# Transposes, values and scores of a tile as one group on TensorE, with attention further ahead

## The chip, the cores and the metric

The kernel runs on one core of a Trainium2 chip. The time is device microseconds of one execution, taken as the median of several runs; lower is better. The engines of a core work side by side, each on its own queue in order: TensorE (PE; its weight loads are listed apart as PEld), VectorE (DVE), ScalarE (ACT), GpSimd (POOL) and SyncE (SP), which here only issues loads. [...]

## The reference

An attention over 4 batches, 8 heads, 768 positions and a head size of 64, in which each query sees the 31 keys nearest to it and, for each of the 24 blocks of 32 positions, one key (the maximum over the block) and one value (the mean). Its output is the input of a two-layer network over 3072 tokens.

```python
k_sum = k.reshape(B, H, nb, block, D).max(axis=3)
v_sum = v.reshape(B, H, nb, block, D).mean(axis=3)
scores_l = scale * np.matmul(q, k.transpose(0, 1, 3, 2))
mask_l = np.abs(pos[:, None] - pos[None, :]) < window
scores_s = scale * np.einsum('bhsd,bhnd->bhsn', q, k_sum) + np.log(block)
a = softmax(concat(where(mask_l, scores_l, -1e9), scores_s))
x = matmul(a, concat(v, v_sum))              # to (3072, 512)
h = x @ w_in                                 # (3072, 1024)
solu = h * softmax(h)
ln = (solu - mean) / sqrt(var + 1e-6) * g_ln
out = ln @ w_out                             # (3072, 512)
```

All is in float32.

## The kernel before

**Tiles and steps.** The network's tokens go in 24 tiles of 128 (t = 0 to 23). Attention goes in 12 pieces (batch b, piece g of 256 queries) of two steps each (pp = 0 or 1, four heads each), 24 steps in all, so one step for a tile of the network; a piece with both of its steps is the input of two tiles. Names in the views carry these numbers: `s2_1_0` is the scores of b = 2, g = 1, pp = 0, and `h12` belongs to tile 12. Steps and tiles are counted from 0.

**Products on TensorE.** For a step: `s`, the scores (16 products in two passes, 32 records of 64x120); `t`, 16 transposes of the normalised weights `e`; `x`, the values (32 records). For a tile: `h` (24 products of 128x512, from the high and low parts `xh`, `xl` of x and of `w_in`), `lt` (16 transposes of the normalised hidden layer `he`) and `o` (24 products of 128x512 with `w_out`). `h` and `o` are called the large products below, the others the small ones. `vs_ps` holds the block means of a batch's values.

**Between them.** Scores: VectorE adds the mask and takes the maximum (8 instructions, `e`, `nm`), ScalarE exponentiates (8 instructions), ScalarE and VectorE make the reciprocal `z`, VectorE or GpSimd multiplies (`e<-e,z`). Transposes `t` are copied to `at` (two copies), `x` to `xh` with a subtraction into `xl`. Hidden layer: VectorE takes the maximum (`hm`), ScalarE exponentiates (`he`, `hz`), VectorE multiplies (`he<-h,hz,he`, the last reader of `h`), then follow mean, variance and a power on GpSimd (`y`). `lt` is copied to `lh`, with a subtraction into `ll`, in two halves each.

**Buffers.** In PSUM `h` has one buffer; `s`, `t`, `lt` and the block means share two in turn; `x` and `o` share two in turn. In SBUF `qt`, `vt`, `kw`, `e`, `at`, `xh`, `lh` have two each and `kraw` three.

**What sets the order.** The kernel is written as a list of operations (`plan.op`), each with a cost, its engines and what it reads and writes. `Plan.issue` then plays a schedule with these costs, takes at each point the operation that can start first (of equals the one that is due first), and issues the instructions in that order, which each engine keeps. So a line that moves in the loop changes the order of all engines. An operation enters the list of those ready when what it depends on has ended, plus `SYNC` (0.13). `run` takes several generators and makes one TensorE operation of their first products. The loop over t (line 724) puts, for a tile, the values and scores of a coming step, the loads (`load_q`, `load_v`, `load_keys`), the first layer (`first`), the transposes (`turn`, `values_turn`), four stages of splitting `w_out` for the first tiles, and the second layer of tile t - 3 (`LAG`). From t = `NEAR` = 4 on the transposes of both kinds go in one `run`, and values and scores in another.

Early on VectorE, ScalarE and GpSimd also split the two weight matrices into high and low parts (`raw`, `cv_in`, `cv_out`, `w`) and form block maxima (`ksum`) and block sums (`st_v`, `vacc`) of the coming batches.

## Time and profile before

| | us |
|---|---|
| median of 3 runs | 418.68 (418.41 to 419.27) |
| the profiled execution | 419.72 |
| its span | 417.9 |
| TensorE, products busy | 396.2 |
| VectorE busy | 284.1 |
| ScalarE busy | 243.6 |
| GpSimd busy | 124.2 |

The profiled execution gives one record for each instruction, with its start, its length and what ended the idle time ahead of it. Ends of products are modelled, so two large products that follow each other overlap in the records, and distances are best read from start to start. A row of the timeline joins neighbours of a kind; `x32` is their count, and a bracket names the idle time ahead of the row and what ended it. The granted clock is TensorE's, 1.00 at full speed.

### The profile page before, as it was taken

What the parts mean: (1) busy time and instruction counts of PE and PEld (TensorE: products, weight loads), DVE (VectorE), ACT (ScalarE), POOL (GpSimd) and SP (SyncE); (2) the same over time, 40 slices, a digit from 0 to 9 for tenths busy, and PEclk for the clock granted to TensorE, in tenths of its full rate; (3) what the DMA queues carried; (4) which work ended last, traced back from release to release, by engine and by line L of the source; (5) the groups of instructions that cost most, each with busy time, mean ns of one, the idle gap of its engine ahead of it and who ended that gap; (6) DMA issues with size and microseconds to landing.
All of it is one profiled execution on the core that took longest, in us unless ns stands there. A gap on an engine that the chain in (4) does not pass through costs nothing.

```text
span 417.9 us, 9489 instructions
## 1 busy us (share of the span) xinstructions
PE 396.2 (95%) x3667; PEld 299.3 (72%) x3667; DVE 284.1 (68%) x841; ACT 243.6 (58%) x710; POOL 124.2 (30%) x172
## 2 busy tenths in 40 slices
PE   7999598889899999999999999999999999999996
PEld 3437376567678777777877777777777777777876
DVE  4998899996877776736876764564676567453440
ACT  4967889737556745745763673675675566332231
POOL 4676546887851101108102110110110100111010
PEclk9999879999999999999999999999999999999999
DMA  8999996428337412126134220241230000000011
GB/s 268 410 256 263 327 245 164 127 78 197 91 117 200 130 49 80 52 88 153 55 100 124 77 78 27 76 102 40 77 95 29 25 6 23 27 25 2 25 50 52
DMA packets 22929, 46.03 MB, mean 110 GB/s; under 512 B 1860, under 2 KB 8260, under 8 KB 22884
## 3 DMA queue, kind: packets, MB, share of 16 engines
q1 hardware_dynamic: 18096, 36.97, 31.4%
q10 hardware_dynamic: 4788, 8.46, 6.2%
q8 instruction: 29, 0.48, 0.5%
q14 instruction: 16, 0.13, 0.1%
HBM read 36.97 MB, written 6.29 MB: 104 GB/s over the span
## 4 chain that ended last, share of the span: by engine, by line
PE 58%; DMA 16%; DVE 15%; ACT 5%; POOL 3%; issue 1%; SPq 0%; DVEq 0%
PE h L616 26%; PE o L681 22%; DMA kraw<-in_k 4%; DMA vt<-in_v 4%; DMA raw<-in_w_out 4%; DVE hm L623 3%; DVE e L518 3%; DVE he L629 3%; ACT he L625 3%; PE x L590 3%; PE lt L552 3%; DMA st_v<-in_vb 2%; PE t L552 2%; PE s L498 2%; POOL st_v L418 2%; DMA raw<-in_w_in 2%
## 5 line engine op out<-in xcount | busy, mean ns | idle before, releaser
L616 PE MATMUL h<-w,xh 128*128 128x512 f32 x384 | 141.1, 405 | 8.2 <-DVE he L629 6.9
L681 PE MATMUL o<-w,lh 128*128 128x512 f32 (+1 forms) x400 | 142.4, 394 | 0.1
L616 PEld LDWEIGHTS h<-w,xh 128*128 128x128 f32 x384 | 72.4, 189 | 31.8 <-issue 11.0
L681 PEld LDWEIGHTS o<-w,lh 128*128 128x128 f32 x400 | 74.1, 188 | 19.0 <-issue 2.9
L681 PE MATMUL o<-w,ll 128*128 128x512 f32 (+1 forms) x200 | 77.2, 386 | 0.5 <-DVE ll L666 0.5
L616 PE MATMUL h<-w,xl 128*128 128x512 f32 x192 | 75.7, 394 | 0.0
L526 ACT ACTIVATE e<-e,nm 128x120 f32<-128x120 f32 x192 | 73.0, 384 | 1.1 <-DVE nm L518 1.1
L636 POOL TENSOR_SCALAR he<-he,nmu 128x512 f32<-128x512 f32 x27 | 23.8, 883 | 99.5 <-DVE nmu L632 99.3
L625 ACT ACTIVATE he<-h,hm 128x1024 f32<-128x1024 f32 x24 | 26.7, 1114 | 42.9 <-DVE hm L623 42.8
L238 ACT COPY at<-t 120x512 f32<-120x512 f32 x45 | 24.2, 587 | 41.5 <-PE t L552 41.4
L681 PEld LDWEIGHTS o<-w,ll 128*128 128x128 f32 x200 | 37.6, 188 | 8.0 <-DVE ll L666 0.8
L518 DVE CUSTOM_DVE_ANT_0 e<-s,mask 128x120 f32<-128x120 f32 x192 | 40.5, 275 | 2.8 <-PE s L498 2.8
L616 PEld LDWEIGHTS h<-w,xl 128*128 128x128 f32 x192 | 36.3, 189 | 6.8
L623 DVE TENSOR_REDUCE hm<-h 128x1 f32<-128x1024 f32 x24 | 29.3, 1221 | 14.9 <-PE h L616 14.9
L240 POOL COPY kw<-ksum 128x192 f32<-128x192 f32 (+1 forms) x26 | 9.4, 363 | 100.6 <-PE s L498 79.9
L641 ACT ACTIVATE sq<-he 128x1024 bf16<-128x1024 f32 x24 | 25.4, 1057 | 22.6 <-POOL he L636 20.6
L239 DVE CAST lh<-lt 128x512 fp32r<-128x512 f32 x23 | 15.8, 687 | 32.4 <-PE lt L552 27.1
L666 DVE TENSOR_TENSOR ll<-lt,lh 128x512 fp32r<-128x512 f32 x48 | 31.8, 684 | 8.5 <-ACT lh L238 8.1
L418 POOL TENSOR_TENSOR st_v<-st_v 96x512 f32<-96x512 f32 (+3 forms) x42 | 33.9, 816 | 8.8 <-DMA st_v<-in_vb 6.3
L526 ACT ACTIVATION_READ_ACCUMULATOR e<-e,nm 128x1 f32 x192 | 36.3, 189 | 0.0
L590 PEld LDWEIGHTS x<-at,vt 120*64 120x64 f32 (+1 forms) x768 | 25.4, 141 | 10.4 <-issue 5.2
L629 DVE SCALAR_TENSOR_TENSOR he<-h,hz,he 128x1024 f32<-128x1024 f32 x24 | 30.7, 1278 | 0.2
(79 smaller groups left out, 525.3 us busy)
## 6 DMA issues: line engine op xcount, KB each, us to landing
vt<-in_v SPq DMA_DIRECT2D x12, 768.0 KB, 5.8
kraw<-in_k SPq DMA_DIRECT2D x16, 400.0 KB, 7.5
out<-os ACTq DMA_DIRECT2D x23, 256.0 KB, 2.0
qt<-in_q SPq DMA_DIRECT2D x11, 512.0 KB, 4.0
st_v<-in_vb SPq DMA_DIRECT2D x12, 384.0 KB, 3.7
raw<-in_w_in SPq DMA_DIRECT2D x8, 512.0 KB, 7.1
raw<-in_w_out SPq DMA_DIRECT2D x8, 512.0 KB, 12.0
vt<-vsum ACTq DMA_DIRECT2D x11, 192.0 KB
```

Of the source, the lines that this page charges most:

```text
L238: by = {act: lambda: nc.scalar.copy(out=to(), in_=of()), dve: lambda: nc.vector.tensor_copy(out=to(), in_=of()), pool: lambda: nc.gpsimd.t ...
L418: op(pool, 0.15 + w * 0.0021, lambda w=w, o=o: nc.gpsimd.tensor_tensor(out=o.ap[:n, :w], in0=x.ap[:n, :w], in1=x.ap[:n, w:2 * w], op=ALU.add),
L518: nc.vector.tensor_tensor_reduce(out=e.ap[:, n, :], in0=sc.ap[:, j, (2 * i + up) * KC:(2 * i + up + 1) * KC], in1=mask[:, mi, :], scale=-S ...
L526: nc.scalar.activation(out=e.ap[:, n, :], in_=e.ap[:, n, :], func=AF.Exp, bias=nm.ap[:, n:n + 1], scale=-1.0, accum_out=z.ap[:, n:n + 1])
L590: nc.tensor.matmul(xp.ap[j * D:(j + 1) * D, i, qs], vs.ap[:k, u, cs], at.ap[:k, u % 2, n[j] + u // 2, :], start=not apart, stop=not apart ...
L616: nc.tensor.matmul(o, a.ap[:, c, ts], w.ap[:, i], start=(c == 0 and n == 0), stop=(c == NKC - 1 and n == 2))
L623: op(dve, 1.13, lambda: nc.vector.tensor_reduce(out=nm.ap, in_=h.ap, op=ALU.max, axis=AX.X, negate=True), r=[h], w=[nm])
L625: op(act, 1.09, lambda: nc.scalar.activation(out=e.ap, in_=h.ap, func=AF.Exp, bias=nm.ap, accum_out=z.ap), r=[h, nm], w=[e, z])
L629: op(dve, 1.27, lambda: nc.vector.scalar_tensor_tensor(out=e.ap, in0=h.ap, scalar=z.ap, in1=e.ap, op0=ALU.mult, op1=ALU.mult, accum_out=s1 ...
L641: op(act, 1.13, lambda: nc.scalar.activation(out=sq.ap, in_=e.ap, func=AF.Square, accum_out=ss.ap), r=[e], w=[sq, ss])
L666: op(dve, 0.6, lambda part=part, r=r: nc.vector.tensor_tensor(out=part(lo), in0=tp.ap[:, r], in1=part(hi).bitcast(F32), op=ALU.subtract), ...
L681: nc.tensor.matmul(o.ap[:, cols], a.ap[:, f, :], w.ap[:, i, cols], start=(f == 0 and n == 0), stop=(f == NFC - 1 and n == 2))
```

## The change

The switch `NEAR` goes from 4 to 6. Up to it, scores, transposes and values of a step each are an operation of their own. From tile 6 on a tile's small products are put in this order: transposes of step t + 3 (`values_turn`), transposes of tile t - 2 together with the values of step t + 2, and the scores of step t + 4. They are chained: each carries `then`, the operation that TensorE has to take next, so that nothing comes in between, and the first waits for what the second needs. Scores were one pair of tiles ahead and are now two, and the loads of queries (`load_q`) and keys (`load_keys`, at tables `load_at` and `blocks_at`) are asked for at other tiles. In `Plan.issue` an operation of TensorE that follows one of TensorE no longer has `SYNC` added before it is ready.

```diff
@@ -37,7 +37,7 @@
 NT = B * S // P
 LAG = 3
 NHE = 4
-NEAR = 4
+NEAR = 6
 WPT = 2
 
 
@@ -64,6 +64,7 @@
     def __init__(self, can, deps, prio, nbytes, port):
         self.can, self.deps, self.engine, self.fn, self.port = can, deps, None, None, port
         self.prio, self.nbytes, self.end, self.start, self.users, self.left = prio, nbytes, None, None, [], 0
+        self.then = None
 
 
 class Plan:
@@ -128,7 +129,7 @@
         return o
 
     def issue(self):
-        ready, free, dma = {}, {}, 0.0
+        ready, free, then, dma = {}, {}, {}, 0.0
         for o in self.ops:
             o.left = len(o.deps)
             for d in o.deps:
@@ -138,8 +139,9 @@
             if "sp" in o.can:
                 o.due = o.prio
 
-        def enter(o, at):
+        def enter(o):
             for e in o.can:
+                at = max((d.end + (0.0 if d.engine == e == "pe" else self.SYNC) for d in o.deps), default=0.0)
                 ready.setdefault(e, []).append((at, o))
 
         def begin(e, at):
@@ -154,6 +156,8 @@
 
         def take(e):
 
+            if e in then:
+                return next(((begin(e, at), o) for at, o in ready[e] if o is then[e]), None)
             best = None
             for at, o in ready[e]:
                 t = begin(e, at)
@@ -173,13 +177,16 @@
 
         for o in self.ops:
             if not o.left:
-                enter(o, 0.0)
+                enter(o)
         order = []
         while len(order) < len(self.ops):
             t, e, o = min(((x[0], e, x[1]) for e in ready for x in [take(e)] if x),
                           key=lambda x: (x[0], x[2].due))
             for f in o.can:
                 ready[f] = [x for x in ready[f] if x[1] is not o]
+            then.pop(e, None)
+            if o.then:
+                then[e] = o.then
             o.start, o.engine, (o.cost, o.fn) = t, e, o.can[e]
             o.end = free[e] = t + cost(e, o, t)
             if o.nbytes:
@@ -189,7 +196,7 @@
             for u in o.users:
                 u.left -= 1
                 if not u.left:
-                    enter(u, max(d.end for d in u.deps) + self.SYNC)
+                    enter(u)
         at, done = self.START, set()
         for o in order:
             if o.engine == "pe":
@@ -541,8 +548,10 @@
             cost, fns, r, w = zip(*(x for _, x in mine))
             op(pe, sum(cost) - 0.25 * (len(mine) - 1), lambda: [f() for f in fns],
                r=[x for y in r for x in y], w=[x for y in w for x in y])
+            done = plan.ops[-1]
         for f, _ in mine:
             assert next(f, None) is None
+        return done if mine else None
 
     def turn_halves(to, of):
 
@@ -721,30 +730,57 @@
     for f in range(NFC):
         load_w_out(f, ())
     rows = [(hh, i) for hh in range(2) for i in range(2)]
+
+    load_at, blocks_at = ((0, 1, 2, 3), (-1, 0, 1, 1)), ((0, 1, 2, 3), (0, 1, 1, 2))
+
+    def pairs(at, t):
+        return [(b + 1, p) for b in range(B - 1) for p in range(NPAIR) if t == 2 * NG * b + at[b > 0][p]]
+
+    step = lambda i: (*its[i // 2], i % 2)
     for t in range(NT):
         n, j = divmod(t, 2)
         b, g = its[n]
-        nxt = its[n + 1] if n + 1 < len(its) else None
-        near, before = t >= NEAR, its[(t + 1) // 2:(t + 1) // 2 + 1]
-        run(*[values(*x, (t - 1) % 2) for x in before if near], *([scores(*nxt, j)] if nxt else []))
+        near = t >= NEAR
+        if not near:
+            run(scores(*step(t + 2)))
+
+        if t == NEAR - 1 or (near and j == 0 and n + 3 < len(its)):
+            load_q(*its[n + 3])
+        elif j == 0 and not near:
+            load_q(*its[n + 2], after=begun if n == 0 else ())
         if j == 0 and n + 2 < len(its):
-            load_q(*its[n + 2], after=begun if n == 0 else ())
             load_v(*its[n + 2], after=begun if n == 0 else ())
-        if b + 1 < B and g < 2:
-            load_keys(b + 1, 2 * g + j, begun if n < 2 else ())
+        for p in pairs(load_at, t):
+            load_keys(*p, begun if t < 4 else ())
         first(t)
         rows_behind = [turn(t - LAG + 1)] if t > LAG - 2 else []
-        run(*([values_turn(*nxt, j)] if nxt and near else []), *rows_behind)
+        if near:
+            parts = [run(values_turn(*step(t + 3)))] if t + 3 < NT else []
+            parts.append(run(*rows_behind, *([values(*step(t + 2))] if t + 2 < NT else [])))
+            if t + 4 < NT:
+                parts.append(run(scores(*step(t + 4))))
+
+
+            for x, y in zip(parts, parts[1:]):
+                x.then = y
+                y.deps.add(x)
+            parts[0].deps.update(*[y.deps - {parts[0]} for y in parts[1:2]])
+        else:
+            run(*rows_behind)
         for f in range(WPT * t, min(WPT * t + WPT, NFC)):
             split_w_out(f)
         if t > LAG - 1:
             second(t - LAG)
         if not near:
-            run(values_turn(*nxt, j))
-            if t + 1 < NEAR:
-                run(values(*nxt, j))
-        if b + 1 < B and g < 2:
-            key_blocks(b + 1, 2 * g + j)
+            run(values_turn(*step(t + 2)))
+            if t == NEAR - 1:
+                run(scores(*step(t + 3)))
+            run(values(*step(t + 2)))
+            if t == NEAR - 1:
+                run(values_turn(*step(t + 3)))
+                run(scores(*step(t + 4)))
+        for p in pairs(blocks_at, t):
+            key_blocks(*p)
 
         if b + 1 < B and (g < 2 if b else g == 1):
             for r in [2 * g + j] if b else [2 * j, 2 * j + 1]:
```

Three places show what that does to the order. The first is TensorE around the transposes of tile 11 (`lt11`), behind the last products `h13`, where each tile from 7 to 19 looks alike. Before, in the order of issue:

```order
L616 MATMUL h13_3022<-w5_509,xh2_0_2620 128x512
L552 MATMUL t2_1_1_3065<-ident_66,e2_1_1_2977 120x64 x16
L552 MATMUL lt11_3082<-ident_66,he11_2780 128x64 x16
L616 MATMUL h13_3022<-w7_533,xh2_0_2620 128x512
L616 MATMUL h13_3022<-w7_533,xl2_0_2647 128x512
L616 MATMUL h13_3022<-w7_533,xh2_0_2620 128x512
L681 MATMUL o10_3107<-w8_724,lh10_2918 128x512
L681 MATMUL o10_3107<-w8_724,ll10_2924 128x512
L681 MATMUL o10_3107<-w8_724,lh10_2918 128x512
L590 MATMUL x2_1_1_3114<-at2_1_1_3102,vt2_1_2420 64x64 x16
L498 MATMUL s2_2_0_3131<-kw2_2_0_2792,qt2_2_2622 64x120 x16
L681 MATMUL o10_3107<-w9_740,lh10_2918 128x512
```

TensorE in the changed kernel, at the same `lt11`:

```order
L625 MATMUL h13_3084<-w7_533,xl2_0_2681 128x512
L625 MATMUL h13_3084<-w7_533,xh2_0_2661 128x512
L561 MATMUL t2_2_0_3128<-ident_66,e2_2_0_3056 120x64 x16
L561 MATMUL lt11_3148<-ident_66,he11_2818 128x64 x16
L599 MATMUL x2_1_1_3165<-at2_1_1_3000,vt2_1_2436 64x64 x16
L505 MATMUL s2_2_1_3188<-kw2_2_1_2853,qt2_2_2449 64x120 x16
L690 MATMUL o10_3214<-w8_724,lh10_3023 128x512
L690 MATMUL o10_3214<-w8_724,ll10_3027 128x512
```

All 24 products of `h13` stand ahead of the group, all 24 of `o10` behind it, and behind these all 24 of `h14`; `t` and `s` are one step further ahead than they were.

The second place is VectorE near the maximum of tile 2 (`hm2`) and, some 20 rows on, its last reader of `h2` (`he2`); `raw15` and `cv_out3` are stages of the split of `w_out`, `ksum` are block maxima. VectorE before, first around `hm2`:

```order
L326 TENSOR_SCALAR cv_out3_907<-raw15_151 128x512
L330 SCALAR_TENSOR_TENSOR raw15_151<-raw15_151 128x512
L380 TENSOR_REDUCE ksum1_0_948<-kraw1_0_663 128x24 x2
L623 TENSOR_REDUCE hm2_994<-h2_899 128x1
L358 SCALAR_TENSOR_TENSOR w14_975<-cv_out3_907,g_sb_69,w14_975 128x512
L358 SCALAR_TENSOR_TENSOR w15_1000<-cv_out3_907,g_sb_69,w15_1000 128x512
```

and, behind the eight instructions of the scores `s0_2_1`, around `he2`:

```order
L628 RECIPROCAL hz2_1011<-hz2_1011 128x1
L643 TENSOR_SCALAR ss0_941<-ss0_941 128x1
L380 TENSOR_REDUCE ksum1_1_1075<-kraw1_1_666 128x24
L629 SCALAR_TENSOR_TENSOR he2_1010,s12_1089<-h2_899,hz2_1011,he2_1010 128x1024
L666 TENSOR_TENSOR ll1_1099<-lt1_1046,lh1_1072 128x8x64
```

VectorE in the changed kernel, the same two pieces:

```order
L337 SCALAR_TENSOR_TENSOR raw14_149<-raw14_149 128x512
L333 TENSOR_SCALAR cv_out3_930<-raw15_151 128x512
L632 TENSOR_REDUCE hm2_966<-h2_888 128x1
L337 SCALAR_TENSOR_TENSOR raw15_151<-raw15_151 128x512
L387 TENSOR_REDUCE ksum1_0_994<-kraw1_0_663 128x24
```

and behind the scores `s0_2_1`:

```order
L637 RECIPROCAL hz2_999<-hz2_999 128x1
L365 SCALAR_TENSOR_TENSOR w14_1028<-cv_out3_930,g_sb_69,w14_1028 128x512
L638 SCALAR_TENSOR_TENSOR he2_998,s12_1064<-h2_888,hz2_999,he2_998 128x1024
L365 SCALAR_TENSOR_TENSOR w15_1052<-cv_out3_930,g_sb_69,w15_1052 128x512
L605 TENSOR_TENSOR xl0_2_1085<-x0_2_0_878,xh0_2_1048 128x512
```

`hm2` moved ahead of a `raw` and of both `ksum`, of which one now stands behind `he2`, with `w15` and the `ksum` of the next pair.

The third place is TensorE at the end, around the last transposes (`lt22`, `lt23`). Before:

```order
L681 MATMUL o21_4815<-w10_616,lh21_4782 128x512
L552 MATMUL lt22_4840<-ident_66,he22_4721 128x64 x16
L681 MATMUL o21_4815<-w11_710,lh21_4782 128x512
L681 MATMUL o21_4815<-w11_710,ll21_4788 128x512
L681 MATMUL o21_4815<-w11_710,lh21_4782 128x512
L552 MATMUL lt23_4868<-ident_66,he23_4822 128x64 x16
L681 MATMUL o21_4815<-w12_824,lh21_4782 128x512
```

TensorE in the changed kernel:

```order
L690 MATMUL o21_4834<-w15_1052,ll21_4799 128x512
L690 MATMUL o21_4834<-w15_1052,lh21_4793 128x512
L561 MATMUL lt22_4869<-ident_66,he22_4696 128x64 x16
L561 MATMUL lt23_4889<-ident_66,he23_4801 128x64 x16
L690 MATMUL o22_4917<-w8_724,lh22_4906 128x512
L690 MATMUL o22_4917<-w8_724,ll22_4909 128x512
```

Both transposes now stand behind all of `o21` and right ahead of `o22`, which reads the copies of `lt22`.

## The prediction

> **What bounds the kernel now.** I read the page first: its busy times, then the slices.
>
> ```profile
> PE 396.2 (95%) x3667; PEld 299.3 (72%) x3667; DVE 284.1 (68%) x841; ACT 243.6 (58%) x710; POOL 124.2 (30%) x172
> PEclk9999879999999999999999999999999999999999
> ```
>
> TensorE is busy for 95% of the span, and its clock drops once, in the fifth and sixth slices. A busy PE is not a PE at its peak, so I split the span into windows of 20 us (columns: length, then busy time and instructions of PE, PEld, DVE, ACT and POOL, granted clock, DMA share, GB/s).
>
> ```profile
> 80.00:100.00 20.00, 16.88 (x150) 12.84 (x149) 19.65 (x66) 12.03 (x40) 16.33 (x26) 1.00 0.40 105
> 240.00:260.00 20.00, 19.84 (x194) 15.32 (x194) 11.91 (x36) 10.92 (x31) 1.88 (x3) 1.00 0.18 54
> ```
>
> There are two regimes. Up to about 100 us VectorE is full (19.65 of 20) and PE waits. After that PE is full and VectorE is at 60%. The changed code acts in both, because it also moves rows of tiles 1 to 5. The next view is PE's timeline over tile 13, in the second regime (start, us, engine, line, operation).
>
> ```profile
> 240.40 0.40 PE L616 MATMUL h<-w,xh 128*128 128x512 f32 x1
> 240.73 0.69 PE L552 MATMUL t<-ident,e 64*120 64x64 f32 x16
> 241.25 0.67 PE L552 MATMUL lt<-ident,he 64*128 64x64 f32 x16
> 241.85 0.50 PE L616 MATMUL h<-w,xh 128*128 128x512 f32 x1
> 242.19 0.40 PE L616 MATMUL h<-w,xl 128*128 128x512 f32 x1
> ...
> 243.12 0.40 PE L681 MATMUL o<-w,lh 128*128 128x512 f32 x1
> 243.44 1.15 PE L590 MATMUL x<-at,vt 120*64 120x64 f32 x32
> 244.52 1.05 PE L498 MATMUL s<-kw,qt 64*64 64x120 f32 x32
> 245.50 0.50 PE L681 MATMUL o<-w,lh 128*128 128x512 f32 x1
> 245.84 0.40 PE L681 MATMUL o<-w,ll 128*128 128x512 f32 x1
> ...
> 248.15 0.40 PE L681 MATMUL o<-w,lh 128*128 128x512 f32 x1
> 248.71 0.47 PE L616 MATMUL h<-w,xh 128*128 128x512 f32 x1 [0.16 <-DVE he L629]
> 249.02 0.40 PE L616 MATMUL h<-w,xl 128*128 128x512 f32 x1
> ```
>
> Read start to start. From 242.19 to 243.12 lie four gaps between large products: 0.2325 us each, the unit of the rest. A detour through small products shows by what it adds: 240.40 to 242.19 is 1.79 us where two gaps take 0.465, so transposes cost 1.33; 243.12 to 245.84 is 2.72, so values and scores cost 2.26. At 248.71 PE waits for `he`: 248.15 to 249.02 is 0.87 instead of 0.465, **0.40 lost**. The trace's own idle time there is only 0.16, since ends of products are modelled.
>
> **Part 1, one detour instead of two.** Joined out of the same rows: entry 0.33, `t` 0.52, `lt` 0.60, `x` 1.08, `s` 0.98, and 0.34 to the second large product behind it; 3.85 less 0.465 is 3.39, against 1.33 + 2.26 = 3.59. One detour fewer saves 0.20. The step from `lt` to `x` is in no row: `lt` takes 0.60 where a large product follows, `t` 0.52 where another transpose of the same row tiling follows. These are the ends; I take 0.60, since `x` has another tile shape. [...] Behind tile 4 the order has 42 detours before (18 of `t` with `lt`, 17 of `x` with `s`, one `x`, four `lt`, two means) and 28 now, because tiles 4 to 6 are split finer while 14 groups are whole. 14 x 0.20 = **2.8 us less** (ends 1.5, if a lone `lt` is dearer than a paired one, and 3.9).
>
> **Part 2, the wait of `h` for its PSUM.** `h` has one buffer; the next tile may write it when VectorE has read it in `he`.
>
> ```profile
> 247.27 1.28 DVE L629 SCALAR_TENSOR_TENSOR he<-h,hz,he 128x1024 f32<-128x1024 f32 x1
> L616 PEld LDWEIGHTS h<-w,xh x218: 186/188/192, 151.8 to 359.9; 128*128 128x128 f32 x109
> issue: 5.9, 11
> 109.41 0.47 PE L616 MATMUL h<-w,xh 128*128 128x512 f32 x1 [1.19 <-DVE he L629]
> 142.73 0.47 PE L616 MATMUL h<-w,xh 128*128 128x512 f32 x1 [0.66 <-DVE he L629]
> ```
>
> The weight loads of `h` between 152 and 360 us stand idle 11 times, 5.9 us in all: the stall of 248.71 comes in nearly every tile, 11 x 0.40 = 4.4. The two waits above add 1.9. In the changed order all 24 `o` and the whole group lie between the end of one `h` and the next: 24 x 0.2325 + 3.4 = 9.0 us. In tile 13 `he` ended at 247.27 + 1.28 = 248.55, 6.4 us behind the last `h` products (242.19). So these waits go, 4.4 + 1.9 = 6.3; I count **6.0 less**, with ends of 4.0 and 7.0 (4.0 if the queue ahead of `he`, below, eats a part).
>
> **Part 3, what the group puts in a queue.** Four results now fall due at once. Two waits can arise.
>
> ```profile
> 241.46 1.08 ACT L238 COPY at<-t 120x512 f32<-120x512 f32 x2 [3.92 <-PE t L552]
> 251.86 1.16 DVE L245 TENSOR_TENSOR e<-e,z 128x960 f32<-128x960 f32 x1
> L666 DVE TENSOR_TENSOR ll<-lt,lh 128x512 fp32r<-128x512 f32 x48 | 31.8, 684 | 8.5 <-ACT lh L238 8.1
> ```
>
> The scores take the PSUM buffer that this group's `t` has used, so they wait for both copies `at`. These end 241.46 + 1.08 - 240.73 = 1.81 behind the start of `t`; `s` starts 0.52 + 0.60 + 1.08 = 2.20 behind it. 0.39 of room, if ScalarE is free, and the order has `at` ahead of the softmax of `h` there. Second, the group opens with the `t` of the scores of the group before. Before, scores end (245.50) to normalised `e` (253.02) took 7.5. Now VectorE has ahead of the scores' reduction: the maximum of `h` (1.13), a copy `lh`, two `ll`, an `xl` (four of 0.68) and `he` (1.21), 5.1 us and some 0.6 of waits for ScalarE, begun as the group begins; the group itself lasts 3.2. That is 2.5 later, 10.0 in all. The window is 46 x 0.2325 + 0.34 + 0.33 = 11.4. **Cost nothing, with 1.4 us of cover**; when the cover is gone, each us beyond costs 14 us.
>
> **Part 4, the start.** Here VectorE's order decides.
>
> ```profile
> 73.27 1.41 DVE L326 TENSOR_SCALAR cv_out<-raw 128x512 int32<-128x512 int32 x1
> 74.60 1.78 DVE L330 SCALAR_TENSOR_TENSOR raw<-raw 128x512 int32<-128x512 int32 x1
> 76.31 1.80 DVE L380 TENSOR_REDUCE ksum<-kraw 128x24 f32<-128x768 f32 x2
> 78.03 1.21 DVE L623 TENSOR_REDUCE hm<-h 128x1 f32<-128x1024 f32 x1
> 79.16 1.89 DVE L358 SCALAR_TENSOR_TENSOR w<-cv_out,g_sb,w 128x512 fp32r<-128x512 f32 x2
> 83.57 1.27 DVE L629 SCALAR_TENSOR_TENSOR he<-h,hz,he 128x1024 f32<-128x1024 f32 x1
> 84.90 0.50 PE L616 MATMUL h<-w,xh 128*128 128x512 f32 x1 [2.63 <-DVE he L629]
> PE h L616 <- DVE he L629: 4.7, 3, 2.6
> ```
>
> Tile 3 starts at 84.90 because `he` of tile 2 came at 83.57. The maximum `hm` of tile 2 now stands right behind `cv_out`, so at 74.6 rather than 78.03. From it to `he` go, with the new order, `hm` 1.13, one `raw` 1.7, one `ksum` 0.9, the eight reductions 1.6 (the time from 81.05 to 83.57, less a `ksum`) and one `w` 0.95, some 6.3: `he` at 80.9, 2.7 earlier. How much of it reaches tile 5 is in no row: nothing at the least, since VectorE is full and the rows that stand behind now come later; at most the waits of `h` in this stretch, 4.7 us between 57 and 104 us (the last row). Tile 3's own `he` gains too, since it starts earlier and one Pool product that VectorE did (`e` of 0_2_1) is off its queue. I take **3.5 less**, between the 2.7 of the row that it is nearest to and the 4.7.
>
> **Part 5, the loads.** Queries are asked for one pair of tiles earlier, keys of the later batches by another table; both go through SyncE's queue, in which a load waits for its buffer and holds those behind it.
>
> ```profile
> kraw<-in_k SPq DMA_DIRECT2D x16, 400.0 KB, 7.5
> 146.51 0.95 DVE L380 TENSOR_REDUCE ksum<-kraw 128x24 f32<-128x768 f32 x1 [2.74 <-DMA kraw<-in_k]
> ```
>
> Keys take 7.5 us to land, and at 146.51 VectorE stood 2.74 for them. In the new order the keys of (2, second pair) are ahead of the values they were behind, and their `ksum` stands ahead of an `e` on VectorE. I take nothing: two to three tiles (29 us and more) lie between most loads and their use. The ends are that wait of 2.7 gone, and the same wait once on the path.
>
> **Part 6, the end.** `lt22` and `lt23` are now next to each other, with `o22` behind them.
>
> ```profile
> 407.32 0.39 PE L681 MATMUL o<-w,ll 128*128 128x256 f32 x1 [0.49 <-DVE ll L666]
> ```
>
> `o22` must wait for two copies (1.08) and a last `ll` (0.68) behind `lt22`, 1.9 with hand-overs, of which `lt23` covers 0.5: 1.5 of stall, where before 0.49 was lost. **1.1 more** (0.5 to 2.0).
>
> **Sum.** 2.8 + 6.0 + 3.5 - 1.1 = 11.2 less. The profiled execution took 419.72 (span 417.9): 408.5. The median of the runs, 418.68, lies 1.04 below it: **407.5**; a little kept back for waits that I don't see gives 408.0.
>
> **Rivals.** (a) The start gives nothing: VectorE is full there, and what one row gains another loses. 408.0 + 3.5 = 411.5. For it, 19.65 of 20 busy; against it, that PE waits for one row which moves up. (b) The waits return inside the group: `s` behind an `at` that VectorE or a late ScalarE copies, 0.8 us in 14 groups: 11 us, no change. Against it, the 0.39 of room; for it, that it is only 0.39. (c) Slower: the chain from scores to transposes outgrows its 11.4 us window. It has 10.0 by rows; from 12.2 on the kernel is slower, since 0.8 x 14 eats the gain. If `he` and `e` lose 2.9 more to one another in VectorE's queue, 1.5 x 14 = 21: 429. (d) The clock: 3.2 us of small products without a large one.
>
> ```profile
> 31.00:36.50 5.50, 5.50 (x112) 3.66 (x111) 5.50 (x7) 3.61 (x7) 4.24 (x4) 1.00 1.05 211
> 49.60:56.40 6.80, 6.31 (x59) 4.72 (x60) 6.80 (x14) 5.05 (x22) 4.08 (x4) 0.50 1.08 238
> ```
>
> Half clock for 6.8 us loses 3.4; once in each of 14 groups that is 48, and 408 becomes 456. But 112 small products in 5.5 us ran at 1.00; the half clock came behind a real gap. [...] (e) That the change doesn't group is excluded: the order shows the groups from tile 6 on (counted from 0).
>
> **How the numbers follow.** The forecast (404 to 411) 0.62, (a) 0.17, more than the forecast, with the far ends of parts 1, 2, 4 and 6, 0.06; (b) 0.05; (c) 0.08; (d) 0.02. The low end takes the far ends, detours 3.9, waits 7.0, start 4.7, end 0.5: 15.1 less, 403.6, so 403.5. The high end takes (a) with part 2 at 4.0 and part 6 at 2.0, 408.0 + 3.5 + 2.0 + 0.9 = 414.4, so 414.5; that leaves room for most of part 5's wait in the forecast itself. Outside are (b) to (d) and a rest. A measurement of this kernel tells about 0.2% from no change. Faster by over that: 0.62 + 0.17 + 0.06 = 0.85; within it 0.05; slower 0.10.
>
> **What would show it.** PE's timeline should show 3.9 us from the last large product ahead of a group to the second behind it, 14.6 from one group to the next, and no row `h` that waits for `he` behind tile 6. Tile 3's first `h` should stand near 81, the end of tile 4's near 99.5. `s` waiting for `at` would be (b), `t` waiting for `e` (c), a clock under 1.00 behind 110 us (d). Tile 3 at 85 would be (a). What I trust least is part 4.

## The result, and the profile after

The changed kernel takes 413.33 us (median of 4 runs, 412.01 to 415.43), the kernel before 418.98 beside it (418.41 to 419.92): a ratio of 0.987, 95% interval 0.982 to 0.991. Its profiled execution took 413.33 with a span of 411.6, against 419.72 and 417.9. So it is faster, as forecast, but by 6.4 us from profile to profile instead of 11.2. The forecast was 408.0 with a range of 403.5 to 414.5; 413.33 lies in its upper end, above the 404 to 411 that were given the chance of 0.62; rival (a), at 411.5, is nearer to it.

The page of the changed kernel has TensorE's busy time and the granted clock by slice:

```profile
PE 390.9 (95%) x3663; PEld 301.7 (73%) x3666; DVE 284.5 (69%) x849; ACT 234.2 (57%) x704; POOL 120.9 (29%) x170
PEclk9999989999999999999999999999999999999989
```

The share of PE is the same 95%; the busy time fell by 5.3 us. The clock has a second dip, in the last slice but one, which the kernel before has not. PE's timeline of the changed kernel around the group behind `h13` (start, us, engine, line, operation):

```profile
238.34 0.39 PE L625 MATMUL h<-w,xh 128*128 128x512 f32 x1
238.66 0.68 PE L561 MATMUL t<-ident,e 64*120 64x64 f32 x16
239.18 0.66 PE L561 MATMUL lt<-ident,he 64*128 64x64 f32 x16
239.77 1.15 PE L599 MATMUL x<-at,vt 120*64 120x64 f32 x32
240.85 1.05 PE L505 MATMUL s<-kw,qt 64*64 64x120 f32 x32
241.84 0.51 PE L690 MATMUL o<-w,lh 128*128 128x512 f32 x1
242.18 0.39 PE L690 MATMUL o<-w,ll 128*128 128x512 f32 x1
...
247.33 0.39 PE L690 MATMUL o<-w,lh 128*128 128x512 f32 x1
247.56 0.39 PE L625 MATMUL h<-w,xh 128*128 128x512 f32 x1
...
253.16 0.69 PE L561 MATMUL t<-ident,e 64*120 64x64 f32 x16
```

From the last large product ahead of the group to the second behind it: 242.18 - 238.34 = 3.84 (forecast 3.85). From `o` to `h` 0.23, an ordinary gap: `h` no longer waits for `he`. From group to group, by the start of `t`, 14.50 (forecast 14.6). All PE waits of this kernel behind 110 us, as the view of waits groups them (total, times, longest):

```profile
PE o L690 <- ACT lh L245: 1.1, 1, 1.1
PE o L690 <- DVE ll L675: 0.8, 1, 0.8
PE s L505 <- ACT at L245: 0.8, 1, 0.8
PE t L561 <- DVE e L252: 0.2, 1, 0.2
```

Two are at the end, one is rival (b) in one tile of 14, one is rival (c) at 0.2. To see where the time went I mark four points of PE's timeline: the last `h` product of tiles 4, 8 and 20 and the very last product. The stretches between them are called stages below. Before:

```profile
103.02 0.39 PE L616 MATMUL h<-w,xh 128*128 128x512 f32 x1
166.43 0.40 PE L616 MATMUL h<-w,xh 128*128 128x512 f32 x1
348.86 0.39 PE L616 MATMUL h<-w,xh 128*128 128x512 f32 x1
414.44 0.28 PE L681 MATMUL o<-w,lh 128*128 128x256 f32 x1
```

and after:

```profile
102.08 0.40 PE L625 MATMUL h<-w,xh 128*128 128x512 f32 x1
163.52 0.40 PE L625 MATMUL h<-w,xh 128*128 128x512 f32 x1
341.30 0.39 PE L625 MATMUL h<-w,xh 128*128 128x512 f32 x1
408.18 0.28 PE L690 MATMUL o<-w,lh 128*128 128x256 f32 x1
```

Up to tile 4 the change gained 0.94, from there to tile 8 another 1.97, to tile 20 4.65 (182.43 to 177.78), and behind it lost 1.30 (65.58 to 66.88). The steady part did about what was forecast; the start gave a quarter of its forecast of 3.5, and the end took more. The end, in PE's timeline:

```profile
392.00 0.40 PE L690 MATMUL o<-w,lh 128*128 128x512 f32 x1
392.33 1.22 PE L561 MATMUL lt<-ident,he 64*128 64x64 f32 x32
394.66 0.50 PE L690 MATMUL o<-w,lh 128*128 128x512 f32 x1 [1.11 <-ACT lh L245]
395.98 0.80 PE L690 MATMUL o<-w,ll 128*128 128x512 f32 x1 [0.83 <-DVE ll L675]
396.57 1.05 PE L690 MATMUL o<-w,lh 128*128 128x512 f32 x2
...
399.61 0.39 PE L690 MATMUL o<-w,ll 128*128 128x512 f32 x1
```

`o22` waits twice, and then its products stand 0.43 apart instead of 0.23 until 399: from 395.73 to 399.14 the granted clock was 0.50. Its mean from 392 to 399, in a table of windows (length, PE, PEld, DVE, ACT, POOL busy, clock, DMA share, GB/s):

```profile
392.00:399.00 7.00, 5.06 (x42) 3.71 (x41) 2.48 (x4) 2.74 (x5) 0.00 (x0) 0.77 0.10 37
```

The start, from tile 3 to tile 4:

```profile
81.88 0.50 PE L625 MATMUL h<-w,xh 128*128 128x512 f32 x1 [1.69 <-DVE he L638]
...
87.26 0.39 PE L625 MATMUL h<-w,xh 128*128 128x512 f32 x1
...
91.00 0.50 PE L802 MATMUL x<-zero 128*128 128x256 bf16 x3
93.38 0.47 PE L625 MATMUL h<-w,xh 128*128 128x512 f32 x1 [1.87 <-DVE he L638]
...
94.25 1.15 PE L599 MATMUL x<-at,vt 120*64 120x64 f32 x32
95.33 1.07 PE L440 MATMUL vs_ps<-vacc,ident 96*24 96x64 f32 x16
96.33 1.05 PE L505 MATMUL s<-kw,qt 64*64 64x120 f32 x32
```

Tile 3 starts at 81.88 (before 84.90; forecast near 81), 3.0 earlier. VectorE's `he` of tile 3 is 4.3 earlier; before and after:

```profile
96.22 1.27 DVE L629 SCALAR_TENSOR_TENSOR he<-h,hz,he 128x1024 f32<-128x1024 f32 x1
91.94 1.28 DVE L638 SCALAR_TENSOR_TENSOR he<-h,hz,he 128x1024 f32<-128x1024 f32 x1
```

Tile 4 begins as much earlier, at 93.38. Before, it began here:

```profile
97.56 0.50 PE L616 MATMUL h<-w,xh 128*128 128x512 f32 x1 [0.39 <-DVE he L629]
```

But in the changed order PE waits 1.87 for this `he`, and the values, means and scores (94.25 to 97.31, 3.06 us) stand behind that wait, within tile 4. Before, they lay ahead of it. So tile 4 ends only 0.94 earlier.

### The profile page after: what moved, and what is told of

Same layout as the page of the kernel before. It is cut to its first block, busy times and chain, and to the rows that moved or that the text cites. A ratio compares the mean times of both kernels' runs of the same rounds, so it can differ in the third digit from the quotient of the medians.

```text
span 411.6 us, 9468 instructions
## 1 busy us (share of the span) xinstructions
PE 390.9 (95%) x3663; PEld 301.7 (73%) x3666; DVE 284.5 (69%) x849; ACT 234.2 (57%) x704; POOL 120.9 (29%) x170
## 4 chain that ended last, share of the span: by engine, by line
PE 69%; DVE 14%; DMA 13%; ACT 2%; issue 1%; SPq 0%; ACTq 0%; DVEq 0%
PE o L690 31%; PE h L625 25%; PE x L599 4%; DMA raw<-in_w_out 4%; PE s L505 4%; DMA kraw<-in_k 3%; DMA st_v<-in_v 3%; PE lt L561 2%; PE t L561 2%; DMA raw<-in_w_in 2%; DVE ksum L387 2%; DVE e L525 1%; DVE hm L632 1%; DVE w L365 1%; DVE cv_out L333 1%; DVE he L638 1%
## 5 line engine op out<-in xcount | busy, mean ns | idle before, releaser
L625 PE MATMUL h<-w,xh 128*128 128x512 f32 x384 | 126.5, 398 | 7.1 <-DVE he L638 5.2
L690 PE MATMUL o<-w,lh 128*128 128x512 f32 (+1 forms) x400 | 128.9, 395 | 1.1 <-ACT lh L245 1.1
L690 PE MATMUL o<-w,ll 128*128 128x512 f32 (+1 forms) x200 | 78.2, 391 | 0.8 <-DVE ll L675 0.8
L645 POOL TENSOR_SCALAR he<-he,nmu 128x512 f32<-128x512 f32 x23 | 21.0, 913 | 119.0 <-DVE nmu L641 109.4
L245 ACT COPY at<-t 120x512 f32<-120x512 f32 x47 | 25.2, 586 | 46.9 <-PE t L561 45.7
L425 POOL TENSOR_TENSOR st_v<-st_v 96x512 f32<-96x512 f32 (+3 forms) x42 | 32.2, 782 | 11.1 <-DMA st_v<-in_vb 10.5
L599 PE MATMUL x<-at,vt 120*64 120x64 f32 (+1 forms) x768 | 28.5, 226 | 0.2
```

The lines of the kernel that those rows point to most:

```text
L245: by = {act: lambda: nc.scalar.copy(out=to(), in_=of()), dve: lambda: nc.vector.tensor_copy(out=to(), in_=of()), pool: lambda: nc.gpsimd.t ...
L425: op(pool, 0.15 + w * 0.0021, lambda w=w, o=o: nc.gpsimd.tensor_tensor(out=o.ap[:n, :w], in0=x.ap[:n, :w], in1=x.ap[:n, w:2 * w], op=ALU.add),
L599: nc.tensor.matmul(xp.ap[j * D:(j + 1) * D, i, qs], vs.ap[:k, u, cs], at.ap[:k, u % 2, n[j] + u // 2, :], start=not apart, stop=not apart ...
L625: nc.tensor.matmul(o, a.ap[:, c, ts], w.ap[:, i], start=(c == 0 and n == 0), stop=(c == NKC - 1 and n == 2))
L690: nc.tensor.matmul(o.ap[:, cols], a.ap[:, f, :], w.ap[:, i, cols], start=(f == 0 and n == 0), stop=(f == NFC - 1 and n == 2))
```

## The experiments

In the profile of the kernel before the clock was 0.50 from 49.60 to 56.42, in that of the changed one from 50.99 to 54.40 and from 395.73 to 399.14. Other executions held none of such stretches or several (a mean clock of 1.000 in one run of "tile 4 behind", of 0.964 in one of "scores cut off"), and the time moves with them: the six runs of the first experiment go from 410.82 (mean clock 0.996) to 415.66 (0.975). By the mean clocks of all the runs on record, some 120, 3.41 us more at half clock go with about 0.9 us more time, within one kernel. So beside the median of the runs I use stages of each profile, which repeat far better behind tile 8. All in us:

| kernel | last h of tile 4 | 4 to 8 | 8 to 20 | 20 to last product | profiled | median | ratio to before (95%) |
|---|---|---|---|---|---|---|---|
| before | 103.02 | 63.41 | 182.43 | 65.58 | 419.72 | 418.98 | |
| before, again | 103.24 | 63.07 | 182.43 | 65.58 | 419.58 | | |
| changed | 102.08 | 61.44 | 177.78 | 66.88 | 413.33 | 413.33 | 0.987 (0.982 to 0.991) |
| changed, again | 103.61 | 61.25 | 177.71 | 67.03 | 414.76 | 412.62 | 0.986 (0.981 to 0.991) |
| planner's line alone | 103.99 | 59.34 | 179.44 | 67.38 | 415.29 | 417.47 | 0.996 (0.993 to 0.999) |
| group alone | 104.00 | 69.51 | 188.78 | 63.84 | 431.47 | 430.51 | 1.026 (1.019 to 1.033) |
| scores cut off | 102.65 | 65.53 | 179.01 | 65.44 | 417.82 | 420.84 | 1.004 (1.000 to 1.007) |
| cut from tile 7 on | 105.91 | 62.02 | 179.29 | 65.55 | 417.92 | 414.90 | 0.990 (0.985 to 0.995) |
| VectorE loaded | 103.70 | 62.93 | 191.38 | 65.53 | 428.69 | 427.39 | 1.023 (1.018 to 1.028) |
| end reordered | 103.59 | 61.26 | 177.68 | 63.60 | 411.29 | 411.35 | 0.980 (0.975 to 0.985) |
| fillers at the end | 105.44 | 61.29 | 177.65 | 65.55 | 415.11 | | |
| tile 4 behind | 98.35 | 61.95 | 177.83 | 67.05 | 410.34 | 410.26 | 0.984 (0.978 to 0.989) |
| end, tile 4 and copies | 101.76 | 63.18 | 180.97 | 63.60 | 414.66 | 413.07 | 0.987 (0.984 to 0.991) |
| end and tile 4 | 102.82 | 64.46 | 177.60 | 63.60 | 413.63 | 411.74 | 0.980 (0.975 to 0.986) |

### Both kernels once more

No edit. The changed kernel:

> The changed kernel once more, unaltered, as the ground for the three beside it. 413.3 us with a spread of 3 us. The profile should again show the period of 14.6 us from group to group and, ahead of the product group of tile 22, a wait of about 1.3 us followed by about 3.4 us at a clock of 0.50. If the half clock at the end was chance, it is missing here; if it follows from the order, it is there again.

The kernel before:

> The kernel before once more, for a second profile of its start. Runs of one order have put the last h of tile 3 anywhere between 86.9 and 88.7 us. If the start is that loose in the kernel before too, its last h of tile 4 moves by 1 us or more from 102.6, and the 0.7 us by which the two first profiles differ there says little; if it comes within 0.3 of 102.6, the 0.7 is the change's. Behind tile 6 h should wait for he in some 14 tiles, 6 us in all, as before. Time 418.8.

(The 102.6 and the 0.7 of the second expectation were read one or two products too early; by the last `h` they are 103.02 and 0.94.) The stages behind tile 8 repeat within 0.15 for both. The half clock at the end came again. The start of the kernel before repeats within 0.22 (103.02 and 103.24), but that of the changed kernel does not: tile 4 ended at 102.08 and then at 103.61. Five more kernels of the table issue the same order up to tile 5 (scores cut off, cut from tile 7 on, VectorE loaded, end reordered, fillers). In these seven profiles tile 4 ends between 102.08 and 105.91, in the middle at 103.61, and the first `h` of tile 3 stands between 80.97 and 84.17, in the middle at 83.40, where it stood at 84.90 and 84.64 before. So tile 3 is earlier each time, by some 1.4 us, and at the end of tile 4 nothing is left of it. In four of the seven a half clock falls into the small products behind the wait for `he`, and from the last `h` of tile 3 to that of tile 4 it takes 16.3 us instead of 14.8.

### What frees h: the planner's line or the group

First the kernel before with the planner's line alone.

```diff
-        def enter(o, at):
+        def enter(o):
             for e in o.can:
+                at = max((d.end + (0.0 if d.engine == e == "pe" else self.SYNC) for d in o.deps), default=0.0)
...
-                    enter(u, max(d.end for d in u.deps) + self.SYNC)
+                    enter(u)
```

> The kernel before with only the planner's line changed that drops the hand-over between two TensorE steps. Nothing is grouped: transposes of a tile still stand apart from its values and scores, with 18 products between. But its order has each h in one piece and 24 products of o between two of them. Theory, the waits of h (6.0 us) go by that order and not by the group: no h waits for he behind tile 6, the two detours of a tile stay (2.8), the waits inside the group do not arise (1.3), the end waits as in the changed kernel: 413.3 + 2.8 - 1.3 = 414.8. Rival, the group itself is what frees h: the waits stay, and only the start moves: 418.

Then the reverse, the changed kernel with that line put back as it was.

> The changed kernel with the planner's line put back that counts a hand-over between two TensorE steps: all groups stay whole, but products of h and o alternate in threes again, and of o only 21 products and one change of tile lie between the last h of a tile and the first of the next. Theory, the order of the line and not the group frees h: 22 x 0.2325 + 0.3 = 5.4 us stand between, where he comes 5.7 to 7.8 behind the last h; 0.3 to 2.4 of wait, 1.2 in the mean, in at least the five tiles 10 to 14 and more in some others: 10 us or more of waits, 418 to 424. Rival, the group frees h by itself: no such waits, 413. In that case the two parts of the change do not need each other.

The line alone removes every wait of `h` for `he` behind 110 us; what is left there is two waits of `o22` (1.1 and 0.8) and two of `t`, 0.5 and 0.4. Its stage 8 to 20 falls by 2.99 of the 4.65; the other 1.66 come with the group, 0.14 for each of the stage's 12 tiles. The profile of 415.29 is near the 414.8 expected, the median of 417.47 is above it. Where the 2 us between them lie stays open: the other runs left no trace, and the clock does not explain them (0.983 in the profiled run, 0.982 in the mean of all). The group alone is **2.6% slower than before**. PE's waits there behind 110 us, and the gap between the last `h` product of tile 13 and the first of tile 14:

```profile
PE h L624 <- DVE he L637: 8.2, 8, 1.8
PE t L560 <- DVE y L660: 3.4, 1, 3.4
```

```profile
253.67 0.39 PE L624 MATMUL h<-w,xh 128*128 128x512 f32 x1
...
260.12 0.47 PE L624 MATMUL h<-w,xh 128*128 128x512 f32 x1 [1.13 <-DVE he L637]
```

With the hand-over counted, an operation that continues a sum is ready only 0.13 after the last, so the planner takes one of another sum first: `h` and `o` alternate in threes, the group falls ahead of the last three `h`, and only 21 `o` products are left to cover the chain to `he`, where values and scores stood among them before. It was expected to be 418 to 424 and is worse, 430.5: besides `h`, the transposes of one group waited 3.4 us (the second row above; the `e` that they read is next to the record it names), and the clock halved for 6.83 us with that wait. Stage 4 to 8, where this lies, is 8 us longer than in the changed kernel, stage 8 to 20 11 us. So the waits of `h` went by the line, and the group needs the line.

### What a detour costs

Scores are cut off by three `o` products, in 14 tiles:

```diff
-            if t + 4 < NT:
-                parts.append(run(scores(*step(t + 4))))
...
+        mark = len(plan.ops)
         if t > LAG - 1:
             second(t - LAG)
+        if near and t + 4 < NT:
+            one = next(o for o in plan.ops[mark:] if "pe" in o.can)
+            apart = run(scores(*step(t + 4)))
+            for x, y in zip([parts[-1], one], [one, apart]):
+                x.then = y
+                y.deps.add(x)
```

> The scores are cut off the group by three large products: two detours instead of one in 14 tiles, all else in place. Theory, a detour costs 0.20 us by itself: the period goes from 14.6 to 14.8, 14 x 0.20 = 2.8 more, less the one wait of scores for a late copy (0.9): 415.2. No wait of h for he behind tile 6. Rival, joining the detours gives nothing and the whole gain of the steady part came from the waits of h: 412.4 to 413.3, period 14.6 or less. Rival, the cut brings the waits of h back: 418.

A miss by the median, 420.84. The edit did more than it was meant to: in the seventh tile 15 products of `o` had covered a wait, and the chain now put them behind it; `t` waited 2.8 us there, a half clock came with it, and the stage 4 to 8 grew by 4.3. The profiled run is the second lowest of twelve, and where the other 3 us of the median lie no profile shows; the clock is not all of it (0.979 in the profiled run, 0.977 in the mean). PE's timeline of a later tile shows the cut by itself:

```profile
243.04 0.40 PE L625 MATMUL h<-w,xh 128*128 128x512 f32 x1
243.37 0.69 PE L561 MATMUL t<-ident,e 64*120 64x64 f32 x16
243.90 0.66 PE L561 MATMUL lt<-ident,he 64*128 64x64 f32 x16
244.49 1.15 PE L599 MATMUL x<-at,vt 120*64 120x64 f32 x32
245.57 0.50 PE L690 MATMUL o<-w,lh 128*128 128x512 f32 x1
245.91 0.40 PE L690 MATMUL o<-w,ll 128*128 128x512 f32 x1
246.14 0.40 PE L690 MATMUL o<-w,lh 128*128 128x512 f32 x1
246.47 1.05 PE L505 MATMUL s<-kw,qt 64*64 64x120 f32 x32
247.45 0.50 PE L690 MATMUL o<-w,lh 128*128 128x512 f32 x1
247.78 0.40 PE L690 MATMUL o<-w,ll 128*128 128x512 f32 x1
```

Detours of 2.87 (243.04 to 245.91) and 1.64 (246.14 to 247.78), less two gaps of 0.2325 each, make 3.58; the whole group 3.84 - 0.465 = 3.375. **0.20 for a detour**, the forecast's number. The same cut from the eighth tile on (`t > NEAR` in place of `near`) leaves that place alone:

> The cut of the scores from the group, from the eighth tile on, so that the seventh keeps its order (its transposes waited 2.8 us in the first kernel with the cut, since the products that covered them stood behind). Theory, a detour costs 0.15 us (the period of the first kernel with the cut was 14.77 to 14.63 where the whole group has 14.62 to 14.50): 13 x 0.15 = 2.0 more, less the late copy (0.8): 413.8. Rival, the second detour also draws half clocks in the steady part (the first kernel with the cut had a mean clock of 0.975 over its runs, the changed one 0.987): 417 to 420 at a mean clock under 0.98.

414.90 is 1.1 above the theory and below the rival's 417; its runs had a mean clock of 0.983. By the stage 8 to 20 it lost 1.58 in 12 tiles, and the wait for the late copy went from 0.7 to 0.2 there: (1.58 + 0.5) / 12 = 0.17. The second detour draws no half clock behind 110 us in this profile.

### How much cover the chain has

Two copies of the scores ahead of each reduction, which overwrites them:

```diff
         def reduce():
+            for _ in range(2 if (b * NG + g) * 2 + pp >= 10 else 0):
+                nc.vector.tensor_copy(
+                    out=e.ap.rearrange("p (a b) k -> p a (b k)", a=2), in_=sc.ap[:, :, :4 * KC])
             for i, j, up in blocks:
```

> Ahead of each reduction of scores from the eleventh on, VectorE copies the scores twice more into e, where the reduction overwrites them: 2.3 us of VectorE in each of 14 groups, all orders unchanged. Theory (part 3), the chain from scores to e has 1.4 us of cover (1.0 to 1.5 by the profile after): each group is late by 2.3 - 1.4 = 0.9, t waits for e in nearly every group, the period goes to 15.5: 412.6 + 12.6 = 425. Rival, other slack takes it (the copies run while VectorE would wait): under 415. Rival, there was no cover: 2.3 x 14 = 32, 445.

427.39, near the theory. The copies took 1.15 each; the wait of `t` is the largest of PE behind 110 us (the `e` that `t` reads is next to the VectorE record that the row names):

```profile
PE t L564 <- DVE y L660: 9.2, 6, 3.1
```

Stage 8 to 20 grew by 13.67, but not evenly. Six of its 12 groups waited for `e`, 1.1 to 3.1 us, and six did not, where nearly every group was expected to; what let those six escape is not shown. Two late loads of `vt` took 1.6. And with the longest wait the clock halved for 6.83 us: that group took 6.06 from its first transposes (310.68) to the second large product (316.74), where 3.52 is usual (238.66 to 242.18 above), 2.5 more. Without the loads and the half clock 9.6 are left, 0.8 for a group in the mean, and 2.31 - 0.8 leaves a cover of 1.5, where the forecast had 1.4. The changed kernel's own profile agrees: there `e` ends 0.9 to 1.7 ahead of `t` in eleven of the thirteen groups behind the first, and 2.9 and 3.5 ahead in the two whose period is longer. The chain from the end of `s` to the end of `e` takes 9.3 to 10.4 us in these (forecast 10.0). Part 3 holds, and rival (c)'s price does roughly.

### The end

`lt22` ahead of `o21`, `lt23` behind it:

```diff
+    run(turn(NT - 2))
     second(NT - LAG)
-    for t in range(NT - LAG + 1, NT):
-        run(turn(t))
-        second(t)
+    run(turn(NT - 1))
+    second(NT - 2)
+    second(NT - 1)
```

> The transposes of tile 22 stand ahead of the 24 products of tile 21, those of tile 23 behind them. Theory, the end lost 3.4 us to its order: a wait of 1.1 for the copies, 0.9 for the second copy and 1.5 by the half clock that followed; one detour more costs 0.2 to 0.3. The clock then stays at 1.00 behind 380 us and the time is 413.3 - 3.1 = 410.2. Rival, the half clock has another cause and comes at the end anyway: only the two waits go, 411.6, and a slice at 0.50 remains behind 385 us. Rival, the end did not matter (the products wait for something else, the last copies): 413.3.

By the profiles 414.76 to 411.29, 3.5 less, and the last stage 67.03 to 63.60, 3.43 less. No wait of `o22` is left, and the clock in the same window is full:

```profile
392.00:399.00 7.00, 7.00 (x44) 5.45 (x43) 1.42 (x3) 1.76 (x3) 0.00 (x0) 1.00 0.10 37
```

By the medians it is 1.3 less, inside the spread of the runs. Then six products of zeros ahead of `o22`:

```diff
             o = plan.buf(ps, [P, DM], F32, "x", 2, f"o{t}")
+            if t == NT - 2:
+                op(pe, 1.2, lambda: [idle(o.ap) for _ in range(6)], w=[o])
...
```

> Six products on a tile of zeros, 512 columns each, stand ahead of the products of tile 22, in the PSUM that these overwrite; the two pairs of transposes stay next to each other. Theory, the half clock at the end comes from the stretch without large products: the fillers fill the wait of 1.1 us, the clock stays at 1.00 behind 380 us, the 24 products of tile 22 take 6.4 us (5.5 and the wait for the second copy) instead of 7.95; 1.5 less by the profile from the end of tile 4 on. Rival, the clock does not go by that stretch: 0.50 for 3.4 us as before, 0.2 more.

The half clock was gone and the last stage 1.48 shorter, as expected. But the planner put the six between `lt22` and `lt23`, and, what matters more, three other kernels of the table whose end is ordered like the changed one's have no half clock there either, without any filler, and the same stage: 65.44, 65.53 and 65.55. So this run shows nothing of fillers. What it and they show is the split of the 3.43: 1.48 (67.03 - 65.55) by the half clock, 1.95 (65.55 - 63.60) by the waits, less the one detour more that the new order has. Of the seven profiles with that end and no filler (with the planner's line alone among them) three have the half clock: the two of the changed kernel and that of the next section.

### The start

The products of tile 4 wait for `x0_2_1` and `s1_0_0`, between which `vs_ps1` stands:

```diff
-            run(scores(*step(t + 2)))
+            small = [last, run(scores(*step(t + 2)))]
...
-        first(t)
+        first(t, small if t == NEAR - 2 else ())
```

(`last` is the operation of the values before, `first` hands the list to its products as `after`.)

> The changed kernel, and the first products of tile 4 stand behind the values, the mean and the scores that were behind them. Theory, the start lost its lead there: PE waited 1.9 us for he of tile 3 with 2.9 us of small products queued behind the wait. They now fill it, the last h of tile 4 comes 1.9 earlier (99.2 to 100.0 instead of 101.0 to 101.9), and since no product up to tile 8 waits, the lead stays: 412.6 - 1.9 = 410.7. Rival, VectorE sets the pace there and the lead is lost at the next wait (transposes waiting for e, or h for he of tile 4): last h near 100, time 412.6.

From the last `h` of tile 3 to that of tile 4 it now took 13.74 (84.61 to 98.35) instead of 14.82: 1.1 of the 1.9 that PE had waited. The earlier end of tile 4, 98.35, is mostly not the edit's: tile 3, which it does not touch, ended 2.65 before the first profile's. Behind tile 4 the stage to tile 8 was 0.5 to 0.7 longer. With the repaired end:

> The changed kernel with the two repairs that worked by their profiles: the transposes of tile 22 ahead of the products of tile 21 (3.5 less) and the first products of tile 4 behind the small ones (1.1 less at tile 4, 0.4 of it left at tile 8). The copies of transposed scores are as in the changed kernel. If the two are separate: 412.6 - 3.5 - 0.4 = 408.7, with no wait of PE over 1 us behind 110 us and a clock of 1.00 there. If the end gives only what its medians gave: 410.9.

Here tile 4 came 1.1 closer to tile 3 again, and the stage from 4 to 8 was 3.2 longer than in the changed kernel's second profile, by these waits among others:

```profile
128.12 0.34 PE L599 MATMUL x<-at,vt 120*64 120x64 f32 x4 [0.80 <-ACT at L245]
...
130.67 1.05 PE L505 MATMUL s<-kw,qt 64*64 64x120 f32 x32 [1.03 <-DVE y L661]
```

411.74 and a ratio of 0.980 are what the repaired end gives alone. The lead at tile 4 was lost at the next waits, as the rival of the run before had it.

The same with the copies of transposed scores on ScalarE alone (`COPY_P[:1]`):

> The changed kernel with the transposes of tile 22 ahead of the products of tile 21, the first products of tile 4 behind the small ones, and the copies of transposed scores on ScalarE alone. If the three losses are separate: 412.6 - 3.1 - 1.9 - 0.9 = 406.7; no wait of PE over 0.5 us behind 110 us and a clock of 1.00 there. If the start gives its lead back: 408.6. If the late copy only moves to ScalarE's queue: 0.9 more than either.

A miss, 413.07. The planner moved the group behind three `o` products, ScalarE then had the exponential of `h` ahead of the copies, and in six tiles the scores waited for them, 3.7 us in all. One of these:

```profile
214.28 1.05 PE L505 MATMUL s<-kw,qt 64*64 64x120 f32 x32 [0.62 <-ACT at L245]
```

Stage 8 to 20 is 3.3 longer. That is rival (b), at 0.6 for each group that it hits, where it was priced at 0.8.

## Why the prediction was right, and where its size was off

**Part 1**, right: a detour costs 0.20 by the timeline, 0.17 by the stages; 14 of them are 2.4 to 2.8, against 2.8. The step from `lt` to `x`, which no row of before held, takes 0.59 (239.18 to 239.77), the 0.60 that was chosen. The 3.9 of the low end is 14 detours at 0.28; no run shows one of that size, they show 0.20 and 0.17.

**Part 2**, right in size. In the stage 8 to 20 nine starts of `h` lost 0.375 each before, 3.4 us (read start to start, as the 0.40 in the prediction), and none does after; three waits, two of them long, gave 2.7 between tiles 4 and 8, 0.4 more came behind tile 20: 6.4 against 6.0. (The last `h` of tile 13 started at 242.42 and not at 242.19, so `he` came 6.1 behind it and not 6.4; beside the 9.0 this changes nothing.) The reason given, that all `o` and the group stand between two `h`, names the order and not what makes it. The planner's line does, and without it the group makes the waits longer. A forecast for the group alone along the same steps would have had the wrong sign.

**Part 3**, right, with a leftover: 0.8 us once for a copy that VectorE made, 0.4 in two smaller places.

**Part 4** failed; I had trusted it least. Its first step held: tile 3 stands 3.0 earlier in the first profile, and earlier in all seven of that order, if by 1.4 in the middle one. The step "how much of it reaches tile 5", taken at 3.5 out of 0 to 4.7, came out as 0.94 at the end of tile 4, and as nothing in the second pair of profiles. The forecast let the lead through because PE would wait less. It did not ask what PE would do in the waits that were left: `he` of tile 3 came 4.3 earlier, but PE came to it earlier still and stood 1.87 with 3.06 of small products queued behind. Moving these out of the way gave 1.1 at tile 4 in three kernels, of which the stage to tile 8 took 0.6 in one and more than all in the other two (one of these with the late copies too). There VectorE, busy for 18.7 of the 20 us from 80 to 100, may set the pace, as rival (a) had it; that is not shown. By its number rival (a) is what happened: 411.5, plus the 1.8 by which the end lost more than forecast, is 413.3. Its sign, tile 3 at 85, did not show.

**Part 5**, nothing, as taken: behind 110 us PE waits for no load. VectorE's waits for keys there fell from 3.8 us in two to 1.5 in one, off the path.

**Part 6** was mis-sized: 1.1 forecast (0.5 to 2.0), and by its own terms 0.9 (1.9 - 0.5 - 0.49). The waits alone cost 1.95 against 0.5 lost before, and in the profiled run the half clock 1.5 on top, some 2.9 in all. The stall was foreseen with 1.5, the half clock only as rival (d), and there in the groups, where no profile of the changed kernel has it: from 163.63 to 167.04 one large product, 32 transposes and 64 other small ones start, with no wait, and the clock stayed at 1.00. In three experiments a half clock did fall into a group, each time with a wait of 2.8 us or more for `e`. At the end of the profiled run it came where transposes, a wait and a second wait follow each other: 3.65 us (392.33 to 395.98) with one large product.

Together, by part: -2.6 (1), -6.4 (2), +1.2 (3), -0.9 (4), +2.9 (6) is 5.8 less; the profiles differ by 6.4, and 0.6 stays without a name. That the time lies within the range owes as much to the range's high end, which was made of rival (a) and a dear end, as to the sum: parts 4 and 6 both missed on the same side, by 2.6 and 1.8.

## What to carry to other kernels

Where a planner sets the order, a change to its rule for ready operations is a change of its own: run it apart from the regrouping it comes with, since here one alone gave 0.4%, the other lost 2.6%, and both together won 1.3%. A gain at a place where an engine is full can come to nothing at the next wait behind it, so look at that wait too, with what is queued behind it. At the end of a kernel look for the last stretch without large products: a short wait there was paid twice where the clock dropped behind it, 1.95 us for the waits and 1.48 for the clock, and it did so in three of seven profiles.

## What the runs showed of the hardware

The half clock came in pieces of 3.41 us, alone (from 50.99 and from 395.73 in the changed kernel's trace) or two in a row (6.83 us from 49.60 in that of before), and the two starts in the changed kernel's trace lie a whole multiple of that apart: 344.74 = 101 x 3.413. With the same order at the end three of seven profiles had the dip there; that it goes by where the waits fall on a grid of such pieces is my estimate from this multiple, and was not shown. In two profiles (changed, again; tile 4 behind) one stretch of this grid, 3.41 us long, held both waits of `o22`, 1.94 us idle, and five large products, and a half clock followed; with the same waits in one stretch and seven or eight large products (planner's line alone, scores cut off) none did. That is not all of it: in the changed kernel the stretch from 392.32 to 395.73 held one large product and 32 transposes and a half clock followed; with VectorE loaded, the stretch from 408.72 to 412.13 held the same and none followed. What decides between these stays open.
